# Turning softmax probabilities by DMA instead of on the matrix engine, with a table moved to GpSimd, in a block-sparse attention and maxout feed-forward kernel

## The chip, the core and the metric

The kernel runs on one core of a Trainium2 chip. The metric is the device time of one execution in microseconds (us): the median of the runs, smaller is better. The engines are called as in the profile: PE (matrix multiply; PEld is its load of weights), DVE (vector), ACT (activation), POOL (GpSimd) and SP (here only an issuer of DMA transfers). Each runs its own list of instructions strictly in the order in which they stand; an instruction that waits holds back all that stand behind it on that engine.

## The reference

```python
B, H, S, D = 4, 8, 768, 64                 # block of 32 rows: 24 blocks
scores = q @ k.T / sqrt(D)                 # masked: only some blocks of keys are seen
mask = |blk_i - blk_j| <= 1 | blk_i in (0, 23) | blk_j in (0, 23) | blk_j in sampled_blocks[blk_i]  # 3 sampled per row
attn = softmax(where(mask, scores, -1e9))
x = (attn @ v) -> [B*S, H*D] = [3072, 512]
h = max(x @ w1, x @ w2, x @ w3)            # 512 -> 768
out = h @ w_out                            # 768 -> 512
```

All is float32 (the sampled blocks are int64); the output is [3072, 512] float32.

## The kernel before

**Numbers as pairs.** Every operand of a large matmul is split into two float16 parts, a high part and a low part (value minus high part), and three products are added in PSUM (`PASSES`: high·high, high·low, low·high). So each tensor that PE reads needs two small steps: a cast to float16, on ACT, and a subtraction, on DVE or POOL.

**Units.** The work of a batch is cut into 12 units, 48 in all. Unit 0 of a batch ("G", global) handles the first and last block of query rows, which see all 768 keys; the other 11 ("sparse") handle two blocks of query rows each, against eight blocks of keys: a window of three, three sampled ones and the two edges. A unit is made of items: a global unit of 4 (128 x 768 scores each), a sparse unit of 2 (128 x 512 scores each). For each item:

1. PE makes scores in `s_ps` (L644 sparse, L687 global), of which there is one buffer.
2. DVE takes the row maximum (L624, L621) and makes the bias (L627).
3. ACT takes exp into `pr`, float32 in SBUF (L653 twice for a sparse item, L695 once for a global one).
4. `probs` (L596 to L615): PE turns `pr` block by block (128 x 128, float32, four to a PSUM bank `tp_ps`, L606), ACT casts the bank to the high part in `pts` (L610), DVE subtracts to make the low part (L612).
5. PE multiplies `pts` with the values (L668 sparse, L707 global) into `av_ps`.

After the last item of a unit DVE divides by the sums (L724 to L726), PE turns the result (L733), ACT and DVE split it (L737, L738) into a quarter of a 256-column buffer `xg`. The values of a sparse unit come through DRAM: V is split into `vhl`, written to `vscr` by SP (L501), and POOL gathers the wanted rows into `vg` by indirect DMA (L585), by the table `rows_of`. The sampled blocks of K are copied into `kg` by DVE, POOL and ACT (L572).

**Feed-forward.** Four units fill an `xg`; then a feed-forward block F (12 in all) runs: 18 groups of 12 matmuls (L760: six slices f of the hidden width times three weights j), with the maximum taken by ACT and DVE (L764, L767), split into `ht` (ACT L770, POOL L771), then 6 groups of 6 matmuls (L781) and a store from SP (L790).

**Weights.** The 24 weight pieces are loaded by SP (L347, L350) into borrowed buffers (`w_stage`, five slots), decoded by POOL and DVE (L354, L358) into `ht[0]` and `ht[1]`, which serve as scratch, scaled (L302 to L307) and split into `w_hl` and `wo_hl` (ACT L381, DVE L383). As the first feed-forward block writes `ht[0]`, it can do 11 of its groups (three buffers `hf`, two banks `f1_ps`) before the last weights have left `ht[0]`, that is before `wo_hl` has been split.

**The order.** All steps are first collected with a cost, a priority and the keys that they read and write (`Plan.add`), and `Plan.order` then makes one list by simulating the engines: each engine takes the ready step of lowest priority number; on PE, feed-forward steps fill the gaps of attention steps. The written order is fixed from then on; the chip follows it whatever the true durations are. The costs in the code are the planner's, and no time in this document is taken from them. In the order of before, the table of rows for the gathers (`rows`, L260 to L283, 23 small DVE steps that need three small loads of the sampled blocks) has priority -4, and the first batch's V has -5.

Of the kernel before, what the change touches and what calls it, by code (L numbers as in the profile page):

```python
# [30 lines left out]
NK, TP, HOLD, WPRI = 2, 0.45, 2.0, 1.0  # L31
# [10 lines left out]
class Plan:  # L42
# [30 lines left out]
    def order(self, hold, switch):  # L73
# [5 lines left out]
        ready, cands, free, last = [0.0] * n, {}, {}, None  # L79
# [13 lines left out]
        while len(out) < n:  # L93
# [15 lines left out]
            if eng == "PE":  # L109
                if op.mode != last:  # L110
                    t += switch
                last = op.mode
# [21 lines left out]
def tile_block_sparse_attention_maxout_ffn(ctx, tc, q, k, v, sampled, w1, w2, w3, w_out, out):  # L134
# [46 lines left out]
    pr = sbuf([P, 768], F32, "pr", 3)  # L181
    pts = sbuf([P, 2 * 768], F16, "pts", 4)
# [37 lines left out]
    def sampled_rows():  # L220
# [34 lines left out]
        for b in range(B):  # L255
            plan.add("SP", 0.6, lambda b=b: Y.dma_start(
                out=vscr[b][S // 2 :].rearrange("o (a x) -> (o a) x", a=2), in_=zero), r=[("ph", 3, 0)], w=[("zrow", b)],
                     land=2.0, pri=-3 + 100 * b)

        def rows():  # L260
            V.tensor_copy(out=val, in_=vi)
            V.tensor_copy(out=blk, in_=rows_of)
            V.tensor_copy(out=o1, in_=oi1)
            V.tensor_copy(out=o2, in_=oi2)
# [616 lines left out]
```

## Time and profile before

| what | value |
|---|---|
| median of 3 runs | 710.01 us (709.4 to 710.67) |
| the profiled execution | 712.67 us |
| its span, first to last instruction | 709.1 us |
| mean granted PE clock | 0.958 |
| PE busy | 636.5 us, 90% |
| DVE, ACT, POOL busy | 441.3, 386.6, 189.1 us |
| DMA queue of SP | 46.28 MB, 24.7% of 16 engines' span |
| DMA queue of POOL | 35.15 MB, 19.0% |

The profiled execution lies 3.57 us above its span, and 2.66 us above the median. Sums in this document are made on the span. The views used are the page (busy time, slices, chain, groups), the windows (busy time of each engine in a stretch of the span), the timeline (instructions in order of time, with the idle time before them and its releaser in brackets), the waits and the DMA issues. A group's row reads: line, engine, operation, out<-in, shape, count, then busy time in us and mean ns of one, then the idle time of the engine just before it.

### The profile page before, as it was taken

What the parts mean: (1) busy time and instruction counts of PE and PEld (TensorE: products, weight loads), DVE (VectorE), ACT (ScalarE), POOL (GpSimd) and SP (SyncE); (2) the same over time, 40 slices, a digit from 0 to 9 for tenths busy, and PEclk for the clock granted to TensorE, in tenths of its full rate; (3) what the DMA queues carried; (4) which work ended last, traced back from release to release, by engine and by line L of the source; (5) the groups of instructions that cost most, each with busy time, mean ns of one, the idle gap of its engine ahead of it and who ended that gap; (6) DMA issues with size and microseconds to landing.
All of it is one profiled execution on the core that took longest, in us unless ns stands there. A gap on an engine that the chain in (4) does not pass through costs nothing.

```text
span 709.1 us, 25850 instructions
## 1 busy us (share of the span) xinstructions
PE 636.5 (90%) x11072; PEld 486.5 (69%) x11072; DVE 441.3 (62%) x1149; ACT 386.6 (55%) x814; POOL 189.1 (27%) x287
## 2 busy tenths in 40 slices
PE   2348456989999999999999999999999999999997
PEld 1236234857788687787787786886886877868784
DVE  1495989787676675577766766675756756652120
ACT  4376767678655765555656545555535545542121
POOL 1122244242321132342211323242311423411110
PEclk9999555979999999999999999999999999999999
DMA  9599699247354292533521534242603414320000
GB/s 214 158 309 259 190 281 271 56 104 157 109 131 92 74 273 64 138 86 95 139 65 45 161 88 122 77 106 80 138 2 92 105 50 123 80 75 17 16 16 30
DMA packets 91237, 83.08 MB, mean 117 GB/s; under 512 B 55273, under 2 KB 76778, under 8 KB 91122
## 3 DMA queue, kind: packets, MB, share of 16 engines
q1 hardware_dynamic: 81266, 46.28, 24.7%
q0 software_dynamic: 9856, 35.15, 19.0%
q8 instruction: 86, 1.41, 0.9%
q14 instruction: 29, 0.24, 0.1%
HBM read 68.72 MB, written 12.70 MB: 115 GB/s over the span
## 4 chain that ended last, share of the span: by engine, by line
PE 79%; DVE 5%; ACT 1%; issue 1%; DVEq 0%; ACTq 0%
PE f_ps L760 39%; PE f_ps L781 13%; PE tp_ps L606 8%; PE av_ps L668 6%; PE s_ps L644 5%; PE s_ps L687 2%; PE tp_ps L315 1%; PE tp_ps L733 1%; PE tp_ps L536 1%; PE tp_ps L469 1%; PE av_ps L707 1%; DVE nm L624 1%; ACT pts L610 1%; DVE w_hl L383 1%; DVE pts L612 1%
## 5 line engine op out<-in xcount | busy, mean ns | idle before, releaser
L760 PE MATMUL f_ps<-xg,w_hl 128*128 128x256 f16 x2592 | 303.2, 274 | 0.8 <-ACT hf L764 0.8
L760 PEld LDWEIGHTS <-w_hl 128*128 128x128 f16 x2592 | 252.1, 99 | 41.7 <-issue 9.0
L585 POOL DMA_INDIRECT vg<-vscr,rows_of x88 | 82.5, 938 | 215.1 <-PE av_ps L668 202.3
L653 ACT ACTIVATE pr<-s_ps,nm,qsm 128x256 f32<-128x256 f32 x176 | 91.9, 562 | 51.3 <-DVE nm L627 45.3
L767 DVE SCALAR_TENSOR_TENSOR hf<-f_ps,hf 128x256 f32<-128x256 f32 x144 | 60.6, 421 | 89.9 <-PE f_ps L760 72.8
L771 POOL TENSOR_TENSOR ht<-hf,ht 128x256 f16<-128x256 f32 x72 | 50.0, 695 | 206.3 <-ACT ht L770 205.9
L781 PE MATMUL f_ps<-wo_hl,ht 128*128 128x512 f16 x432 | 99.8, 379 | 0.8 <-ACT ob L787 0.8
L610 ACT CAST pts<-tp_ps 128x512 f16<-128x512 f32 x120 | 65.5, 558 | 49.0 <-PE tp_ps L606 47.3
L612 DVE TENSOR_TENSOR pts<-tp_ps,pts 128x512 f16<-128x512 f32 x120 | 76.8, 649 | 22.1 <-ACT pts L610 21.7
L606 PE MATMUL tp_ps<-ident,pr 128*128 128x128 f32 x448 | 75.3, 296 | 10.3 <-DVE pts L612 6.0
L624 DVE TENSOR_REDUCE nm<-s_ps 128x2 f32<-128x512 f32 x88 | 60.5, 687 | 29.1 <-PE s_ps L644 21.7
L781 PEld LDWEIGHTS <-ht 128*128 128x128 f16 x432 | 41.0, 99 | 46.6 <-issue 4.4
L606 PEld LDWEIGHTS tp_ps<-ident,pr 128*128 128x128 f32 x448 | 52.7, 149 | 16.9 <-DVE pts L612 7.6
L770 ACT CAST ht<-hf 128x256 f16<-128x256 f32 x72 | 29.0, 404 | 59.4 <-DVE hf L767 59.2
L644 PE MATMUL s_ps<-kg,qt 64*32 64x256 f16 x2112 | 48.7, 285 | 9.4 <-ACT pr L653 9.0
L668 PEld LDWEIGHTS <-pts 128*32 128x32 f16 x4224 | 40.9, 97 | 20.5 <-issue 15.6
L764 ACT ACTIVATE hf<-f_ps 128x256 f32<-128x256 f32 x72 | 27.5, 382 | 46.5 <-PE f_ps L760 45.6
L668 PE MATMUL av_ps<-vg,pts 128*32 128x65 f16 (+1 forms) x4224 | 51.3, 198 | 1.7 <-DVE pts L612 1.0
L572 POOL COPY kg<-kt 128x256 f16 x88 | 34.8, 421 | 40.2 <-PE s_ps L644 36.6
L572 ACT COPY kg<-kt 128x256 f16 x88 | 32.0, 406 | 16.4 <-DVE kt L479 13.5
L627 DVE TENSOR_SCALAR nm<-nm,qsm 128x2 f32<-128x2 f32 (+1 forms) x104 | 38.2, 367 | 1.6
L644 PEld LDWEIGHTS <-qt 64*32 64x32 f16 x2112 | 22.0, 92 | 22.6 <-issue 14.8
(110 smaller groups left out, 650.9 us busy)
## 6 DMA issues: line engine op xcount, KB each, us to landing
vscr<-vhl SPq DMA_DIRECT2D x12, 520.0 KB, 6.5
stage<-in_k_dram SPq DMA_DIRECT2D x24, 256.0 KB, 4.9
stage<-in_v_dram SPq DMA_DIRECT2D x12, 512.0 KB, 7.0
kt<-in_moe_w_dram SPq DMA_DIRECT2D x12, 511.0 KB, 5.7
qn<-in_q_dram SPq DMA_DIRECT2D x20, 256.0 KB, 5.9
out_dram<-ob SPq DMA_DIRECT2D x20, 256.0 KB, 2.2
xg<-in_moe_w_dram SPq DMA_DIRECT2D x6, 511.0 KB, 9.0
vg<-vscr SPq DMA_DIRECT2D x16, 130.0 KB, 3.5
```

The lines of the kernel that those rows point to most:

```text
L572: (A.copy if t == 2 else eng.tensor_copy)(out=dst, in_=src)
L585: plan.add("POOL", 1.02, lambda c=c: L.indirect_dma_start(out=vgj[: 6 * HB, c].rearrange("p e h x -> p (e h x)"), out_offset=None, in_=vsc ...
L606: T.transpose(tp_ps[job["bank"]][:, x : x + P], prt[:, c0 + x : c0 + x + P], ident)
L610: plan.add("ACT", 0.59 * w / 512, lambda hi=hi, w=w, job=job: A.copy(out=hi, in_=tp_ps[job["bank"]][:, :w]), w=[("ph", it % 4, c0)], pri=p ...
L612: plan.add("DVE", 0.69 * w / 512, lambda hi=hi, lo=lo, w=w, job=job: V.tensor_tensor(out=lo, in0=tp_ps[job["bank"]][:, :w], in1=hi, op=ALU ...
L624: plan.add("DVE", 0.7, lambda: V.tensor_reduce(out=n[:, 0:2], in_=s_ps.rearrange("p (d x) -> p d x", d=2)[:, :, :256], axis=AX.X, op=ALU.max),
L644: T.matmul(out=s_ps[r * BS : (r + 1) * BS, hd * 512 : hd * 512 + 256], lhsT=q_t[hp, tq, 2 * i + u, q0 + c * BS : q0 + (c + 1) * BS], rhs=k ...
L653: plan.add("ACT", 0.56, lambda hd=hd: A.activation(out=prt[:, hd * 256 : hd * 256 + 256], in_=s_ps[:, hd * 512 : hd * 512 + 256], func=AF.Exp,
L668: T.matmul(out=av_ps[r * BS : (r + 1) * BS, 2 * i + hd, :w], lhsT=pv[:, tp, hd, e, r * BS : (r + 1) * BS], rhs=vgj[:, c, e, h, (D + 2) * t ...
L760: T.matmul(out=pf, lhsT=w_hl[f][:, j, g, wp], rhs=x[:, g, xp, :], start=g == 0 and n == 0, stop=g == G - 1 and n == 2)
L767: plan.add("DVE", 0.42, lambda h=h, pf=pf: V.scalar_tensor_tensor(out=h, in0=pf, scalar=2.0 ** -14, in1=h, op0=ALU.mult, op1=ALU.max), r=[ ...
L781: T.matmul(out=f2_ps, lhsT=hts[:, f, hp, t * P : (t + 1) * P], rhs=wo_hl[f // 3][:, f % 3, wp], start=f == 0 and n == 0, stop=f == NF - 1 ...
```

## The change

The diff does the following.

- **Probabilities of units 8 to 47** are no longer turned on PE. ACT casts `pr` to the high part in a new SBUF buffer `phl`, POOL makes the low part there, and SP issues one transposing DMA that writes both parts, turned block by block, into `pts`. Units 0 to 7 keep the turn on PE. Of the 104 items, 18 stay and 86 move; as a global item is now handled as two halves of 384 columns, there are 74 transfers of eight 128 x 128 blocks (float16) and 24 of six.
- **Buffers**: `pr` and `pts` shrink from 768 to 512 columns, `phl` is new (three buffers).
- **The table of rows** moves from DVE to POOL, rewritten so that duplicates are found by products of differences, with 21 steps and priority 0.4; three of its preparing steps stay on DVE.
- **Keys of the weights** are given by third and by part, so that a feed-forward group waits for the part it reads and not for the whole piece. `POOL_LOW` is empty: the low parts of weights stay on DVE.
- **Order**: V of batch 0 has priority 0.2 (was -5), weights 2.5 + 0.25 g (was 1 + 0.5 g), `w_stage` has four slots (was five), loads of K and V of the next batch wait until unit 3 of the present batch is done, the edges have U + 0.3 (was U). The planner no longer charges a switch between feed-forward and turn on PE.

```diff
-NK, TP, HOLD, WPRI = 2, 0.45, 2.0, 1.0
+NK, NPR, NPH, NPT = 2, 3, 3, 4
+PV, TURNED, POOL_LOW = 0.2, 8, ()
+TP, HOLD, WPRI, WSL = 0.45, 2.0, 2.5, 0.25
...
-        prt, ptt = pr[it % 3], pts[it % 4]
-        for c0 in range(0, n, 512):
...
+        prt, hl, ptt = pr[it % NPR], phl[it % NPH], pts[it % NPT]
+        hk, lk, tk = ("phh", it % NPH), ("phl", it % NPH), ("pt", it % NPT)
+        if pri < TURNED:
...
+            return [tk, ("ptl", it % NPT)]
+        plan.add("ACT", 0.05 + 0.565 * n / 512, lambda: A.copy(out=hl[:, :n], in_=prt[:, :n]), r=[("pr", it % NPR)], w=[hk], pri=pri)
+        plan.add("POOL", 1.2 * n / 512, lambda: L.tensor_tensor(
+            out=hl[:, n : 2 * n], in0=prt[:, :n], in1=hl[:, :n], op=ALU.subtract),
+            r=[("pr", it % NPR), hk], w=[lk], pri=pri)
+        plan.add("SP", 1.5 * n / 512, lambda: Y.dma_start(
+            out=ptt[:, : 2 * n].rearrange("p (n x) -> p n x", x=P),
+            in_=hl[:, : 2 * n].rearrange("p (n x) -> p n x", x=P), transpose=True),
+            r=[hk, lk], w=[tk, ("ptl", it % NPT)], pri=pri - 2, land=1.8, move=1.6 * n / 512)
+        return [tk, ("ptl", it % NPT)]
...
-        plan.add("DVE", 3.5, rows, r=["sbase", "svi"] + [(x, t) for x in ("sv", "so") for t in range(3)], w=["rows_of", ("xr", 1)], pri=-4)
+        plan.add("POOL", 5.0, rows, r=["sbase", "svi"] + [(x, t) for x in ("sv", "so") for t in range(3)], w=["rows_of", ("xr", 1)], pri=0.4)
...
-                 [(y, i, c0) for y in ("xh", "xl") for c0 in range(0, 256, 64)]) for i in (2, 1)]
+                 [(y, i, c0) for y in ("xh", "xl") for c0 in range(0, 256, 64)]) for i in (2,)]
...
-                plan.add("PE", 1.31, mm, r=xk + [("w", f)], w=[("f1", fb)], pri=pri, mode="f")
+                plan.add("PE", 1.31, mm, r=xk + [("w", f, j, t) for t in range(2)], w=[("f1", fb)], pri=pri, mode="f")
...
-        if x == 5 and b + 1 < B:
-            prep_k(b + 1, U + 2)
+        if x == 3 and b + 1 < B:
+            prep_k(b + 1, U + 2, [("unit", U)])
```

**Where instructions stand.** The first place is DVE at the start of the kernel, where the last of six steps that split K of the first batch (`kt`, L479 before, L489 after) stands near two decodes of weights. Before, the steps on `xr_123` are the table; after its 23 steps, of which the middle is left out here, the last K step follows:

```order
L479 SCALAR_TENSOR_TENSOR kt_89<-tp_ps_144,ksm_104,kt_89 128x8x64
L358 SCALAR_TENSOR_TENSOR ht_130<-kt_90,ob_133 128x512
L261 CAST xr_123<-vi 96x24
L262 CAST xr_123<-rows_of 96x24
L263 CAST xr_123<-oi_146 96x24
L264 CAST xr_123<-oi_147 96x24
...
L283 CAST rows_of<-xr_123 96x24
L479 SCALAR_TENSOR_TENSOR kt_89<-tp_ps_143,ksm_104,kt_89 128x8x64
L302 TENSOR_SCALAR vsm_106<-tp_ps_144 128x1
```

The table gone, DVE has the same K step directly behind the decode, and goes on to the copies of edge keys and the first row maximum:

```order
L489 SCALAR_TENSOR_TENSOR kt_89<-tp_ps_147,ksm_104,kt_89 128x8x64
L362 SCALAR_TENSOR_TENSOR ht_133<-kt_90,ob_136 128x512
L489 SCALAR_TENSOR_TENSOR kt_89<-tp_ps_146,ksm_104,kt_89 128x8x64
L306 TENSOR_SCALAR vsm_106<-tp_ps_147 128x1
L310 TENSOR_SCALAR vsm_106<-vsm_106 128x1
L311 RECIPROCAL vsm_106<-vsm_106 128x1
L562 COPY kg_92<-kt_89 128x2x256 x2
L562 COPY kg_93<-kt_89 128x2x256 x2
L636 TENSOR_REDUCE nm_109<-s_ps 128x1
```

What moved: two DVE steps that wait for loads of the sampled blocks (`oi`) no longer stand ahead of the end of K. On POOL the 21 steps stand behind two copies of sampled keys and ahead of the next two, of a cast of weights and of the first four gathers.

The second place is PE in the middle of the first batch, from the scores of the first item of unit 10 (`s_ps<-kg_92`) to its values (the next `av_ps<-vg_94`). One row of each run of like matmuls is shown (a feed-forward group is 12 matmuls with one `f_ps` and one `w_hl`). Before, `tp_ps<-ident,pr_114` is the turn of this item:

```order
L644 MATMUL s_ps<-kg_92,qt_99 32x256
...
L760 MATMUL f_ps_141<-xg_125,w_hl_63 128x256
...
L668 MATMUL av_ps<-vg_95,pts_117 32x65
...
L606 MATMUL tp_ps_143<-ident,pr_114 128x128 x4
...
L760 MATMUL f_ps_140<-xg_125,w_hl_64 128x256
...
L668 MATMUL av_ps<-vg_94,pts_118 32x65
```

After, no turn of `pr` is left in this stretch, and the values of the item stand nine feed-forward groups behind its scores, where they stood four behind:

```order
L659 MATMUL s_ps<-kg_92,qt_99 32x256
...
L776 MATMUL f_ps_143<-xg_128,w_hl_64 128x256
...
L776 MATMUL f_ps_144<-xg_128,w_hl_65 128x256
...
L683 MATMUL av_ps<-vg_95,pts_120 32x65
...
L776 MATMUL f_ps_144<-xg_128,w_hl_66 128x256
...
L683 MATMUL av_ps<-vg_94,pts_121 32x65
```

What moved: the values of an item went back in PE's list relative to its scores, and the turn between them, four matmuls, is gone.

The third place is SP around the loads of the third batch's K (`stage_8x<-in_k_dram`). Before:

```order
L790 DMA out_dram<-ob_132 128x512
L517 DMA qn_96<-in_q_dram 128x8x64
L790 DMA out_dram<-ob_133 128x512
L501 DMA vscr_136<-vhl 128x2080
L430 DMA stage_78<-in_v_dram 128x8x128
L419 DMA stage_83<-in_k_dram 128x8x64 x2
```

After, the same kinds of transfer stand between transposing DMAs (`pts<-phl`), each of which waits for the low part from POOL:

```order
L527 DMA qn_97<-in_q_dram 128x8x64
L626 DMA_TRANSPOSE pts_121<-phl_116 128x8x128
L806 DMA out_dram<-ob_135 128x512
L626 DMA_TRANSPOSE pts_122<-phl_117 128x8x128
L626 DMA_TRANSPOSE pts_119<-phl_118 128x8x128
L806 DMA out_dram<-ob_136 128x512
L626 DMA_TRANSPOSE pts_120<-phl_116 128x8x128
L429 DMA stage_81<-in_k_dram 128x8x64 x2
```

What moved: SP's list grew by 98 transfers that hold back, while they wait, the loads and stores behind them, and that are held back by stores which wait for the end of a feed-forward block.

More of the change, by code (lines that the diff above doesn't have):

```diff
@@ L109, in order @@
             if eng == "PE":
-                if op.mode != last:
+                if (op.mode in "ft") != (last in "ft") or last in "as" and op.mode != last:
                     t += switch
@@ L224, in sampled_rows @@
         xf = xr[1].rearrange("p y d -> p (y d)")
-        val, blk, dup, tmp, first, o1, o2 = (xf[:N, 32 * i : 32 * i + NB] for i in range(7))
+        val, blk, dup, tmp, row = (xf[:N, 32 * i : 32 * i + NB] for i in range(5))
         vi, oi1, oi2, row_in = (sbuf([N, NB], I32, x) for x in ("vi", "oi1", "oi2", "row_in"))
-        zero = pts[3][0:2, : H * VW]
+        zero = pts[NPT - 1][0:4, : H * VW // 2]
         def slot(dst, t, of):
@@ L615, in probs, with turn @@
-        return [(x, it % 4, c) for x in ("ph", "pl") for c in range(0, n, 512)]
+            def turn():
+                for x in range(0, n, P):
+                    T.transpose(tp_ps[job["bank"]][:, x : x + P], prt[:, x : x + P], ident)
+            plan.add("PE", TP * n / 512, turn, r=[("pr", it % NPR), "ident"], free=[tk, ("ptl", it % NPT)], pri=pri, mode="t", take=job)
+            plan.add("ACT", 0.59 * n / 512, lambda: A.copy(out=ptt[:, :n], in_=tp_ps[job["bank"]][:, :n]), w=[tk], pri=pri, drop=job)
@@ new lines, in probs @@
+            plan.add("DVE", 0.69 * n / 512, lambda: V.tensor_tensor(
+                out=ptt[:, n : 2 * n], in0=tp_ps[job["bank"]][:, :n], in1=ptt[:, :n], op=ALU.subtract),
+                r=[tk], w=[("ptl", it % NPT)], pri=pri, drop=job)
+            return [tk, ("ptl", it % NPT)]
[3 more added lines that the diff above has]
+            r=[("pr", it % NPR), hk], w=[lk], pri=pri)
@@ L673, in values, with global_item @@
                             )
-        return ("PE", 0.58, values, keys + VG(j), "a")
-    def global_item(b, i, hd, q_c, pri):
-        it = it_no[0]
-        it_no[0] += 1
+        plan.add("PE", 0.58, values, r=keys + VG(j), w=["av", ("unit", U)], pri=pri, mode="a")
+    def global_item(U, b, i, hd, q_c, pri):
+        its = (it_no[0], it_no[0] + 1)
+        it_no[0] += 2
         q_t, sm = qt[q_c % 2], qsm[q_c % 4]
-        prt, ptt = pr[it % 3], pts[it % 4]
         hp, kt = slice(hd * 64, hd * 64 + 64), kts[b % NK]
@@ L712, in values @@
                         )
[L713 removed]
+        plan.add("PE", 0.7, values, r=keys + VHL + ["vones"], w=["av", ("unit", U)], pri=pri, mode="a")
     un_no = [0]
```

153 lines of the change are left out of this document (73 added, 80 removed).

## Prediction

> **What bounds the kernel now.** I read the slices and windows first, then the chain, then the groups on PE.
>
> ```profile
> PE 636.5 (90%) x11072; PEld 486.5 (69%) x11072; DVE 441.3 (62%) x1149; ACT 386.6 (55%) x814; POOL 189.1 (27%) x287
> PE   2348456989999999999999999999999999999997
> core 0: us, PE busy (x) PEld busy (x) DVE busy (x) ACT busy (x) POOL busy (x), PEclk, DMA share, GB/s
> 0.00:60.00 60.00, 23.53 (x124) 19.03 (x126) 28.94 (x90) 31.95 (x55) 14.06 (x30) 1.00 0.87 228
> 60.00:120.00 60.00, 34.02 (x736) 23.37 (x735) 51.66 (x116) 42.98 (x81) 19.99 (x27) 0.63 0.88 248
> 120.00:180.00 60.00, 56.19 (x1014) 43.53 (x1014) 47.39 (x131) 41.72 (x87) 19.62 (x27) 0.89 0.48 118
> 300.00:420.00 120.00, 120.00 (x2275) 93.53 (x2264) 84.96 (x219) 69.63 (x150) 33.66 (x50) 1.00 0.39 100
> 540.00:660.00 120.00, 119.80 (x2216) 91.46 (x2216) 68.12 (x174) 56.24 (x127) 33.67 (x50) 1.00 0.27 78
> PE f_ps L760 39%; PE f_ps L781 13%; PE tp_ps L606 8%; PE av_ps L668 6%; PE s_ps L644 5%; PE s_ps L687 2%; PE tp_ps L315 1%; PE tp_ps L733 1%; PE tp_ps L536 1%; PE tp_ps L469 1%; PE av_ps L707 1%; DVE nm L624 1%; ACT pts L610 1%; DVE w_hl L383 1%; DVE pts L612 1%
> ```
>
> There are two regimes. Up to 120 us PE is idle more than half the time, at a granted clock of 0.63 in the second 60 us, while DVE is busy 51.66 of 60 us and the DMA share is 0.88: the start is set by DVE and loads. From 180 us on PE is busy in practically every microsecond at clock 1.00, and nothing else is over 71% (DVE 84.96 of 120). There a microsecond taken from PE is a microsecond of the span, as long as what replaces it doesn't make PE wait. The chain says the same: 79% of it is PE, of which the turns of probabilities (L606) are 8%.
>
> **Term 1, turns removed.** Of 104 items 86 move: 74 sparse ones with four turns and 12 global ones with six, 74 x 4 + 12 x 6 = 368 of 448. What one costs, in the windows of this line alone and in the timeline of a saturated stretch:
>
> ```profile
> 180.00:420.00 240.00, 29.74 (x191) 21.12 (x192) 1.00 0.45 114
> 420.00:660.00 240.00, 26.75 (x172) 18.45 (x170) 1.00 0.30 79
> 403.48 0.56 PE L668 MATMUL av_ps<-vg,pts 128*32 128x65 f16 x48
> 403.97 0.66 PE L606 MATMUL tp_ps<-ident,pr 128*128 128x128 f32 x4
> 404.56 0.52 PE L644 MATMUL s_ps<-kg,qt 64*32 64x256 f16 x24
> 408.34 0.60 PE L606 MATMUL tp_ps<-ident,pr 128*128 128x128 f32 x4
> 408.87 0.56 PE L668 MATMUL av_ps<-vg,pts 128*32 128x65 f16 x48
> ```
>
> By busy time (29.74 + 26.75) / 363 = 0.156 us each, 57 us for 368. From start to the start of the next work it is 0.59 and 0.53 us for four, 0.14 each, 52 us: a turn overlaps its neighbours a little. I take 55, between the two. All 368 lie behind unit 8, so in the saturated part.
>
> **Term 2, the way that replaces them.** The new chain of an item is exp, cast on ACT, low part on POOL, transfer on SP, values.
>
> ```profile
> L624 DVE TENSOR_REDUCE nm<-s_ps 128x2 f32<-128x512 f32 x88 | 60.5, 687 | 29.1 <-PE s_ps L644 21.7 <-ACT pts L610 6.9
> L627 DVE TENSOR_SCALAR nm<-nm,qsm 128x2 f32<-128x2 f32 x88 | 34.8, 395 | 1.2
> L653 ACT ACTIVATE pr<-s_ps,nm,qsm 128x256 f32<-128x256 f32 x176 | 91.9, 562 | 51.3 <-DVE nm L627 45.3 <-DVE kg L572 3.4 <-PE f_ps L760 1.5
> L610 ACT CAST pts<-tp_ps 128x512 f16<-128x512 f32 x104 | 60.8, 586 | 48.0 <-PE tp_ps L606 46.2 <-DVE hf L767 1.4
> L612 DVE TENSOR_TENSOR pts<-tp_ps,pts 128x512 f16<-128x512 f32 x104 | 71.2, 685 | 22.0 <-ACT pts L610 21.5
> L771 POOL TENSOR_TENSOR ht<-hf,ht 128x256 f16<-128x256 f32 x72 | 50.0, 695 | 206.3 <-ACT ht L770 205.9
> L760 PE MATMUL f_ps<-xg,w_hl 128*128 128x256 f16 x2592 | 303.2, 274 | 0.8 <-ACT hf L764 0.8
> POOL vg L585 <- PE av_ps L668: 202.3, 41, 11.3
> q1 hardware_dynamic: 81266, 46.28, 24.7%
> stage<-in_k_dram SPq DMA_DIRECT2D x24, 256.0 KB, 4.9
> stage<-in_v_dram SPq DMA_DIRECT2D x12, 512.0 KB, 7.0
> out_dram<-ob SPq DMA_DIRECT2D x20, 256.0 KB, 2.2
> ```
>
> ACT: the cast is the same size, 586 ns, from SBUF instead of PSUM; taken as equal. The exps of global items are halved: 32 of 384 columns instead of 16 of 768, an estimate of a few us in all, hidden on an engine that is 55% busy. DVE loses 74 x 0.685 and 24 smaller ones, about 60 us, off the path. POOL gets 74 low parts of twice the size of L771, 1.39 us, and 24 of 1.04 (both estimates from 695 ns): 128 us on top of 189, which is 317 of some 655, 48%. It fits, but in order: the low parts stand among gathers, which already made POOL wait 202.3 us for the values that free `vg`, 11.3 us at longest.
>
> The transfer itself is not in this trace. Each full one reads and writes 256 KB in eight blocks. From below, the store of 256 KB lands in 2.2 us; from above, 512 KB of V take 7.0; the nearest row is K's load, the same 256 KB on the same queue: 4.9, which I take. In engine time the SP queue spent 24.7% of 709.1 = 175 us for 46.28 MB and 81266 packets, so 0.99 us by bytes, or 2.2 us if it goes in 1024 rows of 256 B. 92 full ones (74 + 24 x 0.75) are then 91 to 202 us on top of (24.7 + 19.0)% of 709.1 = 310: 61 to 78% of 655 us. The Trainium skill's "Advanced Engine Details and Errata" (X-Bar Transpose (TRN2)) says that transposing DMAs go as fast as plain ones, at 350 to 400 GB/s; by that a full one would move in about 0.7 us, below the lower of these ends. No run here shows it yet.
>
> The chain from scores to values is then 0.69 + 0.40 + 2 x 0.56 + 0.59 + 1.39 + 4.9 = 9.1 us, some 10 with hand-offs; 6.4 and 11.2 with the other two landing times. Its cover is PE's own work between scores and values, from the new order with the durations of these rows (a group of 12 at L760: 303.2 / 2592 x 12 = 1.40 us). For the item shown in the section on the change it is 9 groups plus small attention steps, 14.7 us (8.3 before). Over the 86 moved items I get a median of 14 us, 13 items under 10.4, and two as low as 3.8; those low ones stand where a feed-forward block has run out and the next `xg` isn't full, three places in the program. I charge 3 us of new PE idle at each, 9 us. With landing at 2.2 us it is about 0; if the landing time is 7 or POOL is late, up to 30 to 45, see the rivals. SP: 98 issues stand before and among loads and stores. K, V and q are loaded a unit or more ahead, so I price this at nothing, covered by that lead; without it each late load would hold the next batch's scores.
>
> **Term 3, the start.** DVE and PE before:
>
> ```profile
> 24.45 0.68 DVE L358 SCALAR_TENSOR_TENSOR ht<-kt,ob 128x512 int32<-128x512 int32 x1
> 26.94 0.17 DVE L261 CAST xr<-vi 96x24 f32<-96x24 int32 x1 [1.80 <-DMA vi<-in_sampled_blocks_dram]
> 31.48 0.17 DVE L263 CAST xr<-oi 96x24 f32<-96x24 int32 x1 [4.28 <-DMA oi<-in_sampled_blocks_dram]
> 34.10 0.18 DVE L264 CAST xr<-oi 96x24 f32<-96x24 int32 x1 [2.45 <-DMA oi<-in_sampled_blocks_dram]
> 38.34 0.74 DVE L479 SCALAR_TENSOR_TENSOR kt<-tp_ps,ksm,kt 128x512 f16<-128x512 f32 x1
> 39.13 0.59 PE L315 MATMUL tp_ps<-qsm,ones 128*128 128x1 f32 x2 [13.10 <-DVE kt L479]
> 121.58 3.71 PE L760 MATMUL f_ps<-xg,w_hl 128*128 128x256 f16 x24
> 149.72 1.41 DVE L383 SCALAR_TENSOR_TENSOR wo_hl<-ht,w_t,wo_hl 128x512 f16<-128x512 f32 x2
> 153.12 4.98 PE L760 MATMUL f_ps<-xg,w_hl 128*128 128x256 f16 x24
> 53.76 1.10 POOL L585 DMA_INDIRECT vg<-vscr,rows_of  x1 [1.28 <-DMA vscr<-vhl]
> ```
>
> The table's waits for small loads (1.80 + 4.28 + 2.45 = 8.5 us) and its own steps hold the last K step from 25.1 to 38.3, and PE 13.10 us with it. The new order has K's step right behind the decode. On POOL the table is 21 steps of some 0.18 us (as on DVE, L261), 4 us, ahead of the gathers, which then waited for `vscr` and not for the table: nothing lost.
>
> What that is worth at the end of the start is another matter. The first feed-forward block stops after 11 groups until `wo_hl` is split: 149.72 on DVE, 153.12 on PE. From there PE is saturated. In both orders about the same DVE work stands ahead of that first split: summing the rows' durations, 105 us before and 107.5 after. So the gate moves by the idle time taken out of DVE, 8.5 us; later waits on loads (DMA share 0.88) may eat it, and the fuller 13 us is the other end. I take 8, from 0 to 13. V of batch 1 moved behind unit 3 and weights came to lower priority: attention's first units end earlier, but DVE's sum at the gate is the same, so nothing more. One weight slot fewer: four slots of about 9 us from load to decode are 24 pieces in 54 us, covered by 120 us of start. Keys by third let a group go at most one split (0.7 us) earlier: nothing.
>
> **Sum.** 709.1 - 55 - 8 + 9 = 655.1 us of span. The change to the median is the same 54: 710.0 - 54 = 656 us.
>
> **Rivals.**
>
> *A. The chain is longer than its cover (0.18).* Landing 7 us amid gathers, or a low part that waits on POOL behind a gather: every item then needs 13 us and more, about the median of its cover. Some 40 of 86 items short by 1 to 2 us are 40 to 80 us if none of it overlapped; as one late item shifts the next ones with it, I put 20 to 45: 676 to 700 in the end. For: in-order POOL (202.3 us of waits on gathers). Against: those waits were slack time, and covers in the middle of a batch reach 15 to 29 us.
>
> *B. The transposing transfers are the bound, and the kernel is slower (0.08).* They run through one queue; if a transfer blocks the next one for its whole time, the point from which it decides is the time that attention now has: (709 - 130 at the start - 45 after the last item) / 92 = 5.8 us per full transfer. At 7.0 us, V's row, 92 x 7.0 + 175 = 819 us. Against: the same row is a time from issue to landing with others in flight, not a spacing; by engine time 92 transfers cost 202 us at most. The Trainium skill's "VectorE: DVE Perf Modes" (The three transpose paths) speaks against the change: it gives 1309 ns for a 128 x 128 block by DMA and 390 ns on TensorE, and recommends the latter. By it 736 blocks one after the other would be an estimate of 963 us; the trace's 0.14 us per turn on PE shows that such figures for one block alone are not spacings.
>
> *C. It is hidden anyway (0.04).* If attention and not PE set the pace, fewer turns would leave 706 to 711. Against: PE is busy 120.00 of 120 us.
>
> *D. The start gives more (0.12).* The full 13 us and no idle for covers: 709 - 57 - 13 = 639 of span, 640.
>
> The forecast itself (645 to 668) has 0.58.
>
> **Range and chances.** The unknown costs make 709.1 - 57 - 13 = 639 to 709.1 - 52 + 30 = 687 in span, and 640 to 688 on the median. Stretched to hold D and most of A: 636 to 692, leaving out B, C and the rest. Faster by over 0.2% (what a measurement of this kernel can tell, 1.4 us): forecast, A, D and half of C, 0.90; within it 0.02; slower B, 0.08.
>
> **What would show it.** Right: the turns' line has 80 matmuls left; PE stays at 99% between 180 us and the end of attention; the first scores of unit 0 stand near 26 us; the first split of `wo_hl` is near 142; a transfer lands in 2 to 6 us; PE's idle before values (waiting on DMA or POOL) sums to under 15 us. Wrong: PE idle of tens of us before the values; SP issuing for most of the span; transfers landing in over 7 us; the first feed-forward after 121 us.

## The result and the profile after

| | before | after |
|---|---|---|
| median | 710.11 us (4 runs) | 689.45 us (4 runs, 688.4 to 693.98) |
| ratio | | 0.9724, 95% interval 0.9686 to 0.9761 |
| span of the profiled execution | 709.1 us | 687.5 us |
| mean granted PE clock | 0.958 | 0.926 |
| PE busy | 636.5 us | 608.6 us |

The kernel is faster by 20.7 us where 54 were forecast; the span is shorter by 21.6. The page of the changed kernel (busy time, then the slices of 1/40 of the span, then SP's queue with packets, MB and share):

```profile
PE 608.6 (89%) x10704; PEld 455.5 (66%) x10704; DVE 384.2 (56%) x1030; ACT 398.1 (58%) x830; POOL 305.2 (44%) x406
PE   2787597599999998997999978998999969999997
PEclk9985588589999998999999997999999988999999
DMA  9689798335678399989789599979896498576100
q1 hardware_dynamic: 178626, 70.41, 52.3%
```

PE's slices were all 9 from 180 us on, but for the last; now there are 7s, a 6 and 8s in between, and in three places the clock dips with them. The windows of the changed kernel (columns as before: busy us, then clock, DMA share, GB/s), the last row being all of the time behind 160 us. A transfer's time is counted in the stretch in which it starts, so the DMA share of a short stretch can pass 1:

```profile
0.00:60.00 60.00, 38.58 (x452) 28.25 (x456) 38.17 (x101) 38.38 (x69) 23.42 (x54) 0.89 0.83 217
60.00:120.00 60.00, 44.92 (x824) 33.05 (x815) 51.06 (x124) 44.80 (x85) 24.53 (x31) 0.70 0.91 248
120.00:180.00 60.00, 51.97 (x838) 37.16 (x839) 42.41 (x109) 38.69 (x82) 23.88 (x33) 0.81 0.46 116
300.00:420.00 120.00, 108.63 (x2173) 79.74 (x2171) 68.56 (x190) 71.08 (x153) 61.10 (x75) 0.97 0.84 155
540.00:660.00 120.00, 113.50 (x2212) 84.17 (x2211) 53.95 (x152) 58.33 (x130) 56.24 (x69) 0.96 0.61 123
...
160.00:687.50 527.50, 493.15 (x8974) 371.41 (x8971) 262.22 (x724) 287.43 (x621) 243.40 (x302) 0.97 0.74 142
```

The same window of the kernel before:

```profile
160.00:709.10 549.10, 542.80 (x9588) 415.38 (x9586) 328.52 (x859) 285.78 (x627) 140.71 (x212) 1.00 0.36 92
```

Idle time of PE behind 160 us went from 6.3 us (549.10 - 542.80) to 34.4, and the clock from 1.00 to 0.97.

**An account at 160 us.** Every kind of matmul gets the time from start to start that it had in the saturated part of the kernel before (0.112 us for a matmul of the hidden feed-forward layer, 0.136 for a turn, and so on), and the matmuls that stand behind 160 us are counted in each trace. Before, 496.8 us of work other than turns and 376 turns (51.2 us) were left, 548.0 in all, and took 549.1: 1.1 us lost. After, 482.7 us were left, and took 527.5: **44.8 us lost**. So the 21.6 us are 14.1 from the start, 51.2 from the turns, and 43.7 given back: 28 of them as idle time and the other 16 as matmuls that took longer. The lower clock accounts for most of these 16, not all: 0.03 of 527.5 us is 16 only if PE had been busy throughout. (Of the 376 turns 368 are the ones removed, 50.0 us; the other 8 are now done before 160 us.)

**Where they are lost.** First the waits of PE behind 160 us in the changed kernel (total us, times, longest):

```profile
PE s_ps L659 <- ACT pr L668: 11.6, 9, 2.0
PE av_ps L683 <- DMA pts<-phl: 4.2, 4, 1.5
PE tp_ps L749 <- DVE qsm L306: 2.3, 2, 1.5
```

The largest isn't for the transfers: scores (L659) wait for the exp (L668) that empties `s_ps`. The timeline of PE between feed-forward blocks 5 and 6 shows what that looks like:

```profile
403.81 2.75 PE L797 MATMUL f_ps<-wo_hl,ht 128*128 128x512 f16 x12
...
406.72 0.52 PE L659 MATMUL s_ps<-kg,qt 64*32 64x256 f16 x24
408.76 0.56 PE L683 MATMUL av_ps<-vg,pts 128*32 128x65 f16 x48 [1.53 <-DMA pts<-phl]
409.73 0.52 PE L659 MATMUL s_ps<-kg,qt 64*32 64x256 f16 x24 [0.41 <-ACT pr L668]
411.94 0.38 PE L319 MATMUL tp_ps<-qsm,ones 128*128 128x1 f32 x2 [1.69 <-DVE nm L642]
413.11 0.84 PE L659 MATMUL s_ps<-kg,qt 64*32 64x256 f16 x24 [0.79 <-ACT pr L668]
...
416.24 0.84 PE L659 MATMUL s_ps<-kg,qt 64*32 64x256 f16 x24 [1.51 <-ACT pr L668]
417.01 0.69 PE L749 MATMUL tp_ps<-ident,xr 128*128 128x128 f32 x2
...
419.26 1.04 PE L776 MATMUL f_ps<-xg,w_hl 128*128 128x256 f16 x4
```

One block ends at 406.4, the next can't begin before the last of its four units is turned (417.01), and between them attention runs alone, one item every 3.1 us (413.11 to 416.24): scores, maximum, bias, two exps, then the next scores into the one buffer. The same stretch stands at 255 to 265 and 557 to 570. These are the three places that the prediction named, each at the end of a batch; they cost 5.7, 8.2 and 8.2 us beyond their work, in order of time. The clock falls in them, here in the first:

```profile
255.00:257.00 2.00, 1.85 (x77) 1.08 (x75) 0.29 (x1) 1.09 (x3) 1.19 (x3) 1.00 0.83 221
257.00:260.00 3.00, 1.17 (x56) 0.72 (x60) 2.13 (x11) 1.94 (x4) 0.81 (x3) 0.76 0.84 175
260.00:263.00 3.00, 1.49 (x61) 0.99 (x49) 1.44 (x6) 1.79 (x4) 2.55 (x3) 0.50 0.75 49
263.00:266.00 3.00, 3.00 (x62) 2.35 (x62) 2.53 (x6) 2.56 (x7) 1.87 (x4) 0.60 0.89 163
266.00:270.00 4.00, 4.00 (x103) 3.42 (x100) 1.60 (x3) 1.17 (x4) 1.16 (x1) 1.00 1.20 233
```

At 0.50 the scores of an item take 0.84 instead of 0.52 us (413.11 and 406.72 above). The Trainium skill's "TensorE: Matmul & The Clock Gate" (Part 1: The HAM clock gate) names two usual states of the clock, half and full, set by how busy PE has been recently. The trace agrees: 1.00, then 0.50, with values between them only in stretches in which the clock changes.

The start answers to its rows in the timelines of PE and DVE:

```profile
25.79 1.49 PE L701 MATMUL s_ps<-kt,qt 64*64 64x256 f16 x12
87.77 4.40 PE L776 MATMUL f_ps<-xg,w_hl 128*128 128x256 f16 x23 [0.69 <-DVE xg L754]
139.56 2.74 DVE L393 SCALAR_TENSOR_TENSOR wo_hl<-ht,w_t,wo_hl 128x512 f16<-128x512 f32 x4
143.79 2.78 PE L776 MATMUL f_ps<-xg,w_hl 128*128 128x256 f16 x24
```

Feed-forward begins at 87 instead of 121 and goes on at 143.8 instead of 153.1. DVE's time ahead of the first split of `wo_hl`, before and after (DVE busy us, then clock, DMA share, GB/s):

```profile
0.00:149.72 149.72, 104.27 (x276) 0.83 0.78 213
0.00:139.56 139.56, 105.77 (x265) 0.75 0.79 217
```

DVE has 1.5 us more work there than before and is idle for 33.8 us instead of 45.5. The new way's own costs on POOL and ACT, from the groups by shape:

```profile
L623 POOL TENSOR_TENSOR phl<-pr,phl 128x512 f16<-128x512 f32 x74 | 85.8, 1160 | 97.4 <-issue 82.8 <-ACT phl L622 11.7 <-POOL ht L787 1.6
L622 ACT CAST phl<-pr 128x512 f16<-128x512 f32 x74 | 45.8, 619 | 1.8
```

And from the DMA issues, the last number being the median time to landing:

```profile
pts<-phl SPq DMA_TRANSPOSE x98, 4.8
stage<-in_k_dram SPq DMA_DIRECT2D x24, 256.0 KB, 8.8
```

The low part takes 1160 ns for 512 columns, the cast 619. A transfer lands in 4.8 us; K's loads take 8.8 us instead of 4.9 among them.

### The profile page after: what moved, and what is told of

Its sections match the earlier page's. It is cut to its first block, busy times and chain, and to the rows that moved or that the text cites. A ratio compares the mean times of both kernels' runs of the same rounds, so it can differ in the third digit from the quotient of the medians.

```text
span 687.5 us, 25385 instructions
## 1 busy us (share of the span) xinstructions
PE 608.6 (89%) x10704; PEld 455.5 (66%) x10704; DVE 384.2 (56%) x1030; ACT 398.1 (58%) x830; POOL 305.2 (44%) x406
## 3 DMA queue, kind: packets, MB, share of 16 engines
q1 hardware_dynamic: 178626, 70.41, 52.3%
## 4 chain that ended last, share of the span: by engine, by line
PE 74%; DVE 11%; DMA 5%; ACT 4%; issue 4%; SPq 1%; POOL 0%; DVEq 0%; ACTq 0%; POOLq 0%
PE f_ps L776 41%; PE f_ps L797 11%; PE s_ps L659 6%; PE av_ps L683 5%; DMA pts<-phl 4%; DVE nm L639 2%; PE s_ps L701 2%; PE tp_ps L546 2%; PE tp_ps L479 2%; PE tp_ps L749 2%; PE tp_ps L615 1%; PE av_ps L723 1%; DVE vhl L507 1%; DVE nm L642 1%; ACT pr L668 1%
## 5 line engine op out<-in xcount | busy, mean ns | idle before, releaser
L623 POOL TENSOR_TENSOR phl<-pr,phl 128x512 f16<-128x512 f32 (+1 forms) x98 | 107.8, 1100 | 138.8 <-issue 91.5
L668 ACT ACTIVATE pr<-s_ps,nm,qsm 128x256 f32<-128x256 f32 x176 | 91.8, 562 | 74.8 <-DVE nm L642 63.7
L595 POOL DMA_INDIRECT vg<-vscr,rows_of x88 | 84.8, 964 | 62.8 <-PE av_ps L683 44.1
L683 PEld LDWEIGHTS <-pts 128*32 128x32 f16 x4224 | 42.8, 100 | 34.5 <-issue 17.8
L683 PE MATMUL av_ps<-vg,pts 128*32 128x65 f16 (+1 forms) x4224 | 54.0, 202 | 12.5 <-DVE pts L618 5.6
L659 PE MATMUL s_ps<-kg,qt 64*32 64x256 f16 x2112 | 51.0, 297 | 11.8 <-ACT pr L668 11.6
L622 ACT CAST phl<-pr 128x512 f16<-128x512 f32 (+1 forms) x98 | 58.0, 592 | 4.9 <-DMA pts<-phl 2.4
L582 POOL COPY kg<-kt 128x256 f16 x88 | 35.1, 419 | 45.8 <-PE s_ps L659 40.8
L659 PEld LDWEIGHTS <-qt 64*32 64x32 f16 x2112 | 23.1, 94 | 22.7 <-issue 13.7
L780 ACT ACTIVATE hf<-f_ps 128x256 f32<-128x256 f32 x72 | 27.5, 382 | 18.2 <-PE f_ps L776 16.8
L642 DVE TENSOR_SCALAR nm<-nm,qsm 128x2 f32<-128x2 f32 (+1 forms) x104 | 35.3, 339 | 2.4
L711 ACT ACTIVATE pr<-s_ps,nm,qsm 128x384 f32<-128x384 f32 x32 | 20.9, 668 | 25.3 <-DVE nm L642 19.5
L803 ACT ACTIVATE ob<-f_ps,vsm 128x512 f32<-128x512 f32 x24 | 16.4, 684 | 25.6 <-PE f_ps L797 25.6
```

What stands on the lines that cost most here:

```text
L582: (A.copy if t == 2 else eng.tensor_copy)(out=dst, in_=src)
L595: plan.add("POOL", 1.02, lambda c=c: L.indirect_dma_start(out=vgj[: 6 * HB, c].rearrange("p e h x -> p (e h x)"), out_offset=None, in_=vsc ...
L622: plan.add("ACT", 0.05 + 0.565 * n / 512, lambda: A.copy(out=hl[:, :n], in_=prt[:, :n]), r=[("pr", it % NPR)], w=[hk], pri=pri)
L623: plan.add("POOL", 1.2 * n / 512, lambda: L.tensor_tensor(out=hl[:, n : 2 * n], in0=prt[:, :n], in1=hl[:, :n], op=ALU.subtract), r=[("pr", ...
L659: T.matmul(out=s_ps[r * BS : (r + 1) * BS, hd * 512 : hd * 512 + 256], lhsT=q_t[hp, tq, 2 * i + u, q0 + c * BS : q0 + (c + 1) * BS], rhs=k ...
L668: plan.add("ACT", 0.56, lambda hd=hd: A.activation(out=prt[:, hd * 256 : hd * 256 + 256], in_=s_ps[:, hd * 512 : hd * 512 + 256], func=AF.Exp,
```

## The experiments

In all later comparisons the kernel before took 722.8 to 723.7 us, against 710 in the first, so kernels are compared by their ratio to it, 95% intervals in brackets; 0.01 is 7.2 us. Why they all take longer there isn't known. Two numbers go with each. The **lead** is counted in the written order: how many items have their scores on PE ahead of a feed-forward block's first group, beyond those of the units that this block and the ones before it take in, as a mean over blocks 1 to 10 (of 0 to 11). It is 5.9 items in the kernel before and 3.0 in the changed one. **Lost** is the account above: time behind 160 us beyond the work that is left. It is read from one trace, and runs of one kernel lie up to 8 us apart, so a few us of it tell nothing. The changed kernel lost 44.8 us in the first comparison and 56.2 in a later one. Of the kernel before there is no later trace, so its 1.1 us doesn't stand beside the losses below.

**HOLD.** `Plan.order` lets an attention step on PE wait behind feed-forward groups for up to HOLD us of the planner's time. The first run takes that away:

```diff
-TP, HOLD, WPRI, WSL = 0.45, 2.0, 2.5, 0.25
+TP, HOLD, WPRI, WSL = 0.45, 0.0, 2.5, 0.25
```

> HOLD 0 instead of 2: attention's steps on PE go ahead of feed-forward whenever one is ready, so that units are finished earlier and feed-forward groups are left over to cover the chain. The changed kernel has 28 us of PE idle after the first split of wo_hl and some 11 us of matmuls at a lower clock behind those gaps. Theory 1 (the written order uses up feed-forward too early and leaves attention's chain bare): idle falls under 8 us, most of the 11 us go with it, 655 to 668 us. Theory 2 (chain too long or transfers too slow on the chip, whatever the order): the gaps move but stay, 682 to 692 us.

Measured 0.9385 [0.9363, 0.9406]; lead 6.5, lost 29.3. Theory 1's value (as 710 x 0.9385 = 666), though not its idle time: under 8 us were expected, 23.0 are left. PE's waits behind 160 us:

```profile
PE av_ps L683 <- issue: 6.7, 17, 0.6
PE av_ps L683 <- DMA pts<-phl: 2.4, 1, 2.4
PE s_ps L659 <- ACT pr L668: 2.0, 3, 1.4
```

And its window behind 160 us:

```profile
160.00:678.40 518.40, 495.44 (x9081) 367.44 (x9079) 270.98 (x731) 286.63 (x629) 244.78 (x307) 1.00 0.75 146
```

The wait of scores for exp has gone from 11.6 us (14.1 in the later trace of the changed kernel, below) to 2.0, and the clock is back at 1.00, with the same transfers at the same DMA share. The other idle time (518.40 - 495.44 in all) stands in many small waits.

**All turns back on PE**, with the rest of the change, at HOLD 2 and at HOLD 0:

```diff
-PV, TURNED, POOL_LOW = 0.2, 8, ()
+PV, TURNED, POOL_LOW = 0.2, 48, ()
```

> All probabilities turned on PE again, the rest of the change kept (table on POOL, weights by thirds, order of the loads, global items in halves). Theory 1: the start alone gives its 8 to 9 us, and the 12 us of the saturated part are gone: 699 to 704 us. Theory 2 (what was gained is the start, and more of it than read): under 695. If the start gives nothing or its order costs later: 709 to 716 us.

Measured 1.0190 [1.0166, 1.0214]: slower than the kernel before by 14 us, worse than any value expected. Lead 2.8, lost 34.4. So something in the rest of the change costs more than the start gains, and it isn't the new way.

> Turns on PE as in the run before, with HOLD 0. Together with it, the changed kernel and the first run this gives the price of the turns under each order. Theory 1: with the short chain the order matters little (698 to 706 us), so the turns by DMA gain 35 to 45 us at HOLD 0 and only 10 to 14 at HOLD 2. Theory 2: the same 10 to 14 us at both.

Measured 0.9911 [0.9879, 0.9944]; lead 7.1, lost 16.8. My first theory falls in part here: the order matters with the short chain too (1.019 to 0.991), and the turns by DMA are worth 0.045 (33 us) at HOLD 2 and 0.053 (38 us) at HOLD 0, nearly the same.

**The control**, the kernel before with HOLD 0 (the same edit there):

> The kernel before with HOLD 0 alone, the control. It has only 2 us of PE idle after 153 us. Theory 1: nothing to gain, 706 to 714 us. If attention first is simply the better order for any kernel: 685 to 700 us.

Measured 1.0024 [1.0010, 1.0037]; lead 10.9, lost 15.4. HOLD 0 alone is no gain; it gains in the changed order.

**The gate.** What else sets the order is that loads of K and V of the next batch wait for unit 3. The edit takes that wait out and puts K's steps back to their old place in the program, behind unit 5:

```diff
-            prep_v(b + 1, U + 3, [("unit", U)])
-        if x == 3 and b + 1 < B:
-            prep_k(b + 1, U + 2, [("unit", U)])
+            prep_v(b + 1, U + 3)
+        if x == 5 and b + 1 < B:
+            prep_k(b + 1, U + 2)
```

> The changed kernel, HOLD 2, but loads of K and V of the next batch no longer wait for unit 3, and K's steps stand at the place they had before (behind unit 5 in the written program, so as early as buffers allow). As ratio to the kernel before: the changed kernel has 0.972, with HOLD 0 0.939. Theory 1 (the gate bunches the next batch's K and V work into the units behind unit 3, attention falls behind there, feed-forward runs out, and at HOLD 2 attention never catches up): without the gate the gaps go, 0.930 to 0.945. Theory 2 (the longer chain alone bares attention at HOLD 2): 0.965 to 0.980, as it was.

Measured 0.9399 [0.9352, 0.9447], at HOLD 2, in theory 1's range; lead 6.0, lost 22.0. PE waits 4.3 us for exp:

```profile
PE s_ps L659 <- ACT pr L668: 4.3, 5, 1.8
```

Its window behind 160 us has 18.4 us of PE idle time (515.50 - 497.06):

```profile
160.00:675.50 515.50, 497.06 (x9018) 375.91 (x9016) 265.20 (x730) 283.12 (x621) 242.64 (x303) 0.99 0.70 138
```

> As the run before, but all probabilities turned on PE. With the gate that kernel had 1.019. Theory 1: the gate was what cost it, and the start's 8 to 9 us are left: 0.984 to 0.994. If global items in halves with three narrower buffers of pr are what costs: 1.010 to 1.020, as it was.

That is this edit with TURNED = 48. Measured 1.0000 [0.9986, 1.0015]; lead 9.5, lost 17.7. So the gate is what had cost the turned kernel 0.019, but the start's gain isn't left over. The split of `wo_hl` shows why, in the turned kernel with the gate and without it:

```profile
143.92 2.74 DVE L393 SCALAR_TENSOR_TENSOR wo_hl<-ht,w_t,wo_hl 128x512 f16<-128x512 f32 x4
158.74 2.07 DVE L393 SCALAR_TENSOR_TENSOR wo_hl<-ht,w_t,wo_hl 128x512 f16<-128x512 f32 x3
```

DVE's time ahead of it in the same two runs:

```profile
0.00:143.92 143.92, 105.25 (x265) 0.87 0.77 210
0.00:158.74 158.74, 116.00 (x303) 0.75 0.84 220
```

In these comparisons `wo_hl` is split at 156.7 to 158.7 us in the five traces without the gate, at 140.9 to 146.6 in the eleven that have it on K and V in the first batch, and at 148.8 in the control. Without the gate more of attention stands ahead of the split on DVE: 40 steps on `nm` instead of 35, 34 copies of keys instead of 28. The steps that split K and V are the same 12 and 12. So the start's gain is there only with the gate. Without the gate the turns by DMA are worth 0.060, 43 us, close to the forecast's net 46.

> Neither gate nor HOLD. Theory 1: gate and HOLD 2 do harm only together, so this stays at 0.930 to 0.945, as with either alone. If each costs by itself: 0.905 to 0.925.

Both edits. Measured 0.9535 [0.9498, 0.9571]: outside both ranges. Lead 12.9, lost 38.8. More lead than needed isn't free; two runs below return to that.

**The gate for the first batch only:**

```diff
-            prep_v(b + 1, U + 3, [("unit", U)])
-        if x == 3 and b + 1 < B:
-            prep_k(b + 1, U + 2, [("unit", U)])
+            prep_v(b + 1, U + 3, [("unit", U)] if b == 0 else [])
+        if x == (3 if b == 0 else 5) and b + 1 < B:
+            prep_k(b + 1, U + 2, [("unit", U)] if b == 0 else [])
```

> The gate on K's and V's loads kept for the first batch only (where it lets the first split of wo_hl come at 143 instead of 157 us), the other batches as before; HOLD 2. Ratios so far: 0.972 with the gate in every batch, 0.940 without it. Theory 1 (the gate pays at the start and costs in batches 2 and 3, where K's and V's steps are bunched at 288 to 307 and 441 to 460 us): both gains, 0.915 to 0.935. Theory 2 (its harm comes from the first batch's own steps, pushed into the stall at 120 to 136 us): 0.960 to 0.975.

Measured 0.9617 [0.9563, 0.9670]; lead 3.0, lost 42.5. Theory 1 fails, and the value lies in theory 2's range, whose cause no run tests. The early start and a good order behind it can't be had together that simply: this order lets feed-forward begin at 90 us and has only three items in hand from then on.

> As the run before with HOLD 1, so that attention's steps wait less behind feed-forward. Theory 1: if any starved places are left at HOLD 2 they close, 0.912 to 0.930. If HOLD has no part once the gate is off: equal to the run before.

Measured 0.9431 [0.9407, 0.9455]; lead 4.7, lost 36.4.

> The same with HOLD 0. With the gate everywhere HOLD 0 gave 0.939, without any gate 0.954. Theory 1: 0.915 to 0.935. If attention first piles up transfers (the DMA share is 0.87 to 0.96 from 160 to 540 us with HOLD 0) and this is what then limits: 0.940 to 0.955.

Measured 0.9487 [0.9458, 0.9515]; lead 9.9, lost 36.6: in the range set for transfers that pile up, which a plain copy prices below for the order without gate. HOLD still has a part, and the expected sum of both gains doesn't come.

> Gate for the first batch only, HOLD 2, all probabilities turned on PE. With the gate everywhere 1.019, without it 1.000. Theory 1: the start's gain stands alone, 0.978 to 0.990; with the first run of this group it prices the turns at 38 to 48 us. Theory 2: 1.000 to 1.019.

Measured 0.9918 [0.9891, 0.9944], between the two ranges; lead 4.8, lost 15.9. With turns on PE the first batch's gate gains 0.008; with turns by DMA it costs 0.022. So the worth of the turns by DMA is only 22 us in this pair.

**Are the transfers to blame?** A plain copy of the same bytes in place of each, at HOLD 0, in the changed kernel, and with neither gate nor HOLD. The kernel then leaves out the turning for units 8 to 47, and all else stays:

```diff
-            in_=hl[:, : 2 * n].rearrange("p (n x) -> p n x", x=P), transpose=True),
+            in_=hl[:, : 2 * n].rearrange("p (n x) -> p n x", x=P), ),
```

> HOLD 0 (0.939) with each of the 98 transfers as a plain copy of the same bytes between the same buffers: the probabilities of units 8 to 47 aren't turned. It prices the turning itself. If the transfers are covered: 0.930 to 0.942, though a copy should take less engine time (the DMA share of 0.7 to 0.9 between 180 and 540 us falls by 0.2) and land in 2 to 4 us. If late or crowded transfers are what is left of PE's idle time: 0.915 to 0.927.

Measured 0.9323 [0.9303, 0.9343]: 4.5 us less than with transposing transfers, in the range set for covered transfers.

> The changed kernel once more, beside the others' kernel before (723 us there, 710 in the first comparison), so that its trace can be compared with theirs. Ratio 0.965 to 0.980. Every feed-forward block should begin within a few us of the last of its four units, with no unit ready beyond them, and the time lost after 160 us should be at least the 43 us of the first trace.

Measured 0.9738 [0.9681, 0.9794], lost 56.2: the base for the next runs.

> The changed kernel with plain copies in place of the 98 transposing transfers (the probabilities of units 8 to 47 aren't turned), same order, no lead. Theory 1: the bare stretches go at the pace of scores, maximum and exp, with the transfer a minor part: 0.955 to 0.968. Theory 2 (the landing time of 4.8 us is what PE waits for): 0.935 to 0.950.

Measured 0.9754 [0.9724, 0.9783], lost 54.7: nothing gained, so the transfer isn't even the minor part that theory 1 allowed. The changed kernel, taken again, in its window behind 160 us:

```profile
160.00:705.80 545.80, 504.93 (x9049) 378.13 (x9046) 261.88 (x734) 291.19 (x631) 246.11 (x307) 0.97 0.72 139
```

Its longest wait on PE there:

```profile
PE s_ps L659 <- ACT pr L668: 14.1, 14, 2.1
```

Its SP queue on the page:

```profile
q1 hardware_dynamic: 178626, 70.41, 50.6%
```

The same three with plain copies, the window first:

```profile
160.00:704.30 544.30, 504.27 (x9049) 378.97 (x9046) 262.68 (x734) 290.57 (x631) 246.08 (x307) 0.97 0.50 139
```

The wait:

```profile
PE s_ps L659 <- ACT pr L668: 17.7, 16, 2.1
```

The queue:

```profile
q1 hardware_dynamic: 95394, 70.41, 35.1%
```

The DMA share falls from 0.72 to 0.50, and PE waits for the same exps. For comparison, the queue with all turns on PE (the second run above):

```profile
q1 hardware_dynamic: 81282, 46.28, 23.7%
```

> The kernel without gate and with HOLD 0 had a lead of many units and still lost 38 us (0.954), at a DMA share of 0.91 to 0.96. With plain copies (the probabilities of units 8 to 47 aren't turned): if crowded transfers held it, 0.932 to 0.942; if it is the order, with attention's chain run bare while feed-forward piles up behind it, 0.947 to 0.955.

Measured 0.9478 [0.9446, 0.9509], lost 30.0 against 38.8 with transposing transfers, at the lower end of the range set for the order. Here, with a lead of 13 items, where the DMA share up to 540 us is 0.91 to 0.96 with transposing transfers and 0.58 to 0.63 with plain copies, a fifth of the loss is the transfers'.

**A lead by force.** Blocks 1 to 10 of the changed kernel begin only when one more unit is done; gate, HOLD and transfers stay:

```diff
-        if U % 4 == 3:
+        for V0 in range(3, 48, 4):
+            late = 1 if 1 <= V0 // 4 <= 10 else 0
+            if U != V0 + late:
+                continue
...
-            feed_forward(F, b, slot, rows)
+            feed_forward(F, bb, slot, rows, [("unit", V0 + late)])
```

> The changed kernel with one thing added to its order: feed-forward blocks 1 to 10 begin only when one unit more than their own four is done, so that attention is always a unit ahead and feed-forward groups are left over when its chain is slow. Gate and HOLD 2 stay. Theory 1 (what bares attention is that it has no lead): 0.950 to 0.963, the gain less some us for building the lead. Theory 2 (the transfers are late, or the chain too long, whatever the lead): 0.970 to 0.985, as the delay costs and nothing is won.

Measured 0.9604 [0.9570, 0.9639], lead 5.4, lost 43.4 against 56.2: to make feed-forward wait makes the kernel faster. That is theory 1's range, but some 14 us short of what HOLD 0 gains, and the wait of scores for exp is still there:

```profile
PE s_ps L659 <- ACT pr L668: 13.7, 9, 2.2
```

Most of it stands between two feed-forward blocks again (at 168, 222, 316 to 320 and 372 to 375 us): the forced wait moves the bare stretches more than it ends them. What it saves is other idle time (35.3 us in all against 40.9) and time at the lower clock (0.98 against 0.97).

**Two tries at the best order**: HOLD 0 with the gate on K alone, and no gate with HOLD 1.5.

> A try at the best order: HOLD 0, with the gate on K's loads alone (V's of the next batch free again). With the gate on both, HOLD 0 gave 0.939. Theory 1 (a lead of one to three units is what is wanted, and this order keeps one): 0.928 to 0.942. If V's steps, earlier now, crowd the start: 0.942 to 0.955.

Measured 0.9524 [0.9494, 0.9555]; lead 8.9, lost 36.0.

> The other try: no gate, HOLD 1.5, between 2 (0.940, lead of one unit) and 0 (0.954, lead of up to eight units). Theory 1: the lead grows by no more than a unit or two: 0.930 to 0.945. If any lower HOLD without the gate runs attention bare as HOLD 0 did: 0.947 to 0.955.

Measured 0.9527 [0.9493, 0.9561]; lead 8.6, lost 36.9. Both miss the order that was looked for and lie in the range of their second theory. With the gate on K alone the split of `wo_hl` stands at 148.5 us, between those with the gate on both and those without. The runs with transposing transfers, by lead:

| run | lead, items | lost, us | ratio |
|---|---|---|---|
| changed kernel | 3.0 | 56.2 | 0.974 |
| gate for the first batch | 3.0 | 42.5 | 0.962 |
| the same, HOLD 1 | 4.7 | 36.4 | 0.943 |
| lead by force | 5.4 | 43.4 | 0.960 |
| no gate | 6.0 | 22.0 | 0.940 |
| HOLD 0 | 6.5 | 29.3 | 0.939 |
| no gate, HOLD 1.5 | 8.6 | 36.9 | 0.953 |
| HOLD 0, gate on K | 8.9 | 36.0 | 0.952 |
| first gate, HOLD 0 | 9.9 | 36.6 | 0.949 |
| no gate, HOLD 0 | 12.9 | 38.8 | 0.954 |

With turns on PE the losses were 34.4 at a lead of 2.8, and 15 to 18 at 4.8 and above. The best two, 0.939 and 0.940, beat both the kernel before and the changed one; the interval of 0.943 overlaps with that of 0.940. The lead alone doesn't set the loss: at 3.0 it was 42.5 in one order and 56.2 in another, and with 8 items and more it was 36 to 39.

## Why the prediction was wrong

**Term 1 was about right in size.** The 368 turns removed come to 50.0 us by start-to-start time (55 forecast, bounds 52 and 57).

**Term 3 held, and for its reason, with one thing unseen.** The split moved by 10.2 us on DVE (149.72 to 139.56) and PE's resumption by 9.3, forecast 8 with bounds 0 and 13; counted as work done by 160 us the start gave 14.1, more than the upper bound. As forecast, the split moved by idle time taken out of DVE: 11.7 us of it went (8.5 to 13 forecast), while the work ahead of the split grew by 1.5 (2.5 forecast). But the work is that small only with the gate: without it 116.00 us stand there instead of 105.25, and the split comes 8 to 10 us later than in the control. The prediction had the gate in its order and gave it no part in this. How much of the idle time is the table's isn't shown, as no run puts the table back on DVE.

**The step that failed is the charge for bare covers:** "I charge 3 us of new PE idle at each, 9 us". It was 43.7. Some 22 us of that are the new way's own by the later pair in this order (56.2 lost with turns by DMA, 34.4 with turns on PE); the rest goes with the changed order, which with turns on PE loses 34.4 where the order without the gate loses 17.7. The durations under the charge were right: landing 4.8 (4.9 taken), low part 1160 ns (1.39), ACT equal (619 ns against 586), POOL 305 us (317), engine time 2.0 us a transfer (0.99 to 2.2). Three things were wrong with the step:

- I charged one late item at each of the three places. When feed-forward has run out, all items up to the next full `xg` run one behind the other at 3.1 us each, and the clock halves: 5.7, 8.2 and 8.2 us, 22 instead of 9.
- I took the cover of each item from the new order and never asked how much was in hand. The order of before has 5.9 items in hand, the new one 3.0; any delay then shows, and another 22 us are lost in small pieces (that these come from the short lead is argued, not shown).
- I priced the loads of K, V and q among the new transfers ("I price this at nothing") and V's move behind unit 3 ("so nothing more") at nothing. The gate that holds these loads back costs 0.034 (0.974 to 0.940) at HOLD 2, net of the 13 us by which the split comes earlier with it.

That PE waits because of the order is shown: HOLD and gate change the waits with the transfers as they are, plain copies in the same order don't. That the lead is what matters in the order is shown in part only, as the forced lead left the wait for exp in place. In the order without the gate the new way loses 4.3 us more than with turns on PE (22.0 to 17.7), within the scatter of the runs, so 9 would have been enough there.

Of the marks set, those for landing, first scores, the split and PE's wait before values (5.8 us for transfers, under 15) held. The one that fell, PE at 99%, was the one that mattered: the idle time stands before scores, where I hadn't looked.

**Rivals.** The time fell into A's range of span (676 to 700), and its picture of late items that push the next ones is nearest; its causes, a landing of 7 us or POOL behind a gather, don't show: a transfer lands in 4.8 us, and PE waits 5.8 us for transfers in all. B is out: 357 us of sixteen engines' time for the whole queue (50.6% of 705.8). C has a truth that I dismissed with PE's 120.00 of 120 us: each feed-forward block of the changed kernel begins 0.9 to 4.8 us behind the turn of its last unit, where before ten of the twelve began 12.9 to 32.2 us behind it. So attention sets the pace there, though PE was full before.

The Trainium skill's "Advanced Engine Details and Errata" (X-Bar Transpose (TRN2)) says that transposing DMAs are as fast as regular ones; by that, transposing would have cost nothing here. The runs differ: SP's queue takes 357 us of sixteen engines' time with 98 transposing transfers, 247 (35.1% of 704.3) with plain copies and 174 (23.7% of 733.9) with neither, so 2.0 us for a full one against 0.8. The Trainium skill's "VectorE: DVE Perf Modes" (Rules for kernel authors) recommends TensorE for a 128 x 128 transpose where PSUM will do as the destination. The four pairs here differ: they are 22 to 43 us faster by DMA, with PE 90% busy (660.6 of 733.9 us) when it turns.

**Open.** Why no order lost less than 22 us, why two orders with a lead of 3.0 lost 42.5 and 56.2, why leads of 8 items and more lose 36 to 39 with transposing transfers (plain copies explain 9 of it in one run), and why the first batch's gate costs 16 us with turns by DMA, were not settled.

## What to carry to other kernels

Work taken off a full engine is worth its whole time only while that engine has other work in hand; here it was worth 22 to 43 of 50 us. Count, in the order as written, how many items the producer is ahead of the filler, before and after, and not only how long each item is covered. When a change removes work from one stage and shifts loads and priorities as well, price the shifts by themselves; here one of them, the gate, cost 14 us with turns on PE and 25 with turns by DMA. If stretches with no filler are left, charge them for every item that runs through them, and at half the clock.

## What the runs showed of the hardware

- A transposing transfer of 256 KB in SBUF took 2.0 us of sixteen engines' time and some 1060 packets (178626 less the 81282 of the turned kernel, over 92 full ones), a plain copy 0.8 us and 153 (from 95394).
- PE's granted clock went from 1.00 (255 to 257 us) to 0.50 (260 to 263) with PE busy for 1.17 of the 3 us between and no single wait over 2.0 us. It was at 1.00 from 266 us on, 1 us after feed-forward had resumed. In the place at 419 us that took longer: 0.50 at 419 to 421 us, 0.64 at 421 to 423, 1.00 at 423 to 425.
